# Windowed attention with a gated projection: weights loaded in head order by 64-row transfers, late masks multiplied on GpSimd, and a new fixed order

## The chip, the cores and the metric

The kernel runs on one core of a Trainium2 chip. Five engines work beside each other: TensorE (PE, matrix multiplies; its weight loads are listed as PEld), VectorE (DVE), ScalarE (ACT), GpSimd (POOL) and SyncE (SP, which here issues every DMA). The metric is the device time of one execution in microseconds; the kernel before has a median of 178.93 us over 3 runs (178.68 to 180.42).

## What is computed

Attention over 8 batches, 8 heads, 576 positions and 64 features per head, followed by a gated linear unit and an output projection. Heads 0 to 3 ("plain") look back over 32 positions, heads 4 to 7 ("dilated") over 128 positions at every fourth one.

```python
scores = scale * np.matmul(q, k.transpose(0, 1, 3, 2))
mask_plain = (rel >= 0) & (rel < window)                                          # window = 32
mask_dil = (rel >= 0) & (rel < window * dilation) & (rel % dilation == 0)          # dilation = 4
scores = np.where(masks[None, :, :, :], scores, -1000000000.0)
attn = softmax(scores); attn_out = np.matmul(attn, v)
x = attn_out.transpose(0, 2, 1, 3).reshape(B, S, H * D)                            # 8 x 576 x 512
for k in range(5):
    gate_pre += conv_w[k] * xp[:, k:k + S, :]                                      # causal, per channel
gate = 1 / (1 + exp(-gate_pre))
out = (gate * (x @ w_val)) @ w_out                                                 # 512 x 512 each
```

## The kernel before

The work is cut into 743 tasks with names, and a written list, ORDER, says in which order they are issued and on which engine each runs (P, A, V, G, S for PE, ACT, DVE, POOL, SP). Each engine works through its own share of the list in that order, so a task that waits holds up everything behind it on its engine. HOMES gives each buffer a number, COUNTS how many buffers of a class there are. The list was made ahead of time; nothing is scheduled when the kernel runs.

The names, where b is a batch, g a pair of batches (a group), k a block of a group, cp a half of the 512 channels:

- Loads on SP: Lqp, Lkp, Lvp (plain q, k, v; v in three or four parts), Lqd, Lkd, Lvd (dilated; for batches 0 and 7 q and k have a second piece Lqr, Lkr), Lwv0, Lwv1 and Lwo0, Lwo1 (256 rows of w_val and of w_out each), Lc. Of the large loads only five are under way at once (DEPTH): each waits for the fifth before it to land.
- Tq and Tk (PE, L402 plain, L465 dilated): transposes of q and k; Eq and Ek (ACT or DVE): their copies out of PSUM.
- For each pair of heads and each half of the positions: S (PE, L334) scores for three blocks of 96 queries against 128 keys; E (ACT, L341) the exponential; M (DVE, L348) the multiply with a mask of zeros and ones; then, for both halves, A (PE, L357) the product with v, which has a column of ones beside it, and N (DVE, L366 and L367) the division by the sum.
- U (POOL or ACT): the cast of dilated v (tile vn). HA to HD (POOL or ACT): for batches below NAT = 4 plain v is loaded unshifted, and ten casts per batch write the shifted copies (tile vw).
- Xp (PE, L429) and Xd (PE, L489): transposes back; Fp and Fd: their copies into xT.
- C (PE, L530) the convolution of a block as 80 small matmuls with diagonal matrices; G (ACT, L542) its tanh; V (PE, L550) the product with w_val, 8 matmuls for each half; Y (DVE, L560) gate times value. A group of 1152 positions is cut into 3 blocks of 384, the last group into 4 blocks of 288. C01 is block 1 of group 0, V000 the first half of block 0 of group 0.
- O (PE, L579) the output for 128 positions, EO (ACT or DVE) its copy, ST (SP) its store.
- Wv and Wo (POOL): casts of the weights to bf16 that also put their rows and columns in the order in which the attention leaves its channels. For w_val six tasks of nine casts, most of them 64 rows by 32 or 64 columns; for w_out two tasks of six casts of 32 or 64 rows by 512 columns.

A number behind a P in ORDER puts that many idle multiplies (L664) ahead of a PE task, to keep PE's clock up.

Of the kernel before, what the change touches and what calls it, by code (L numbers as in the profile page):

```python
# [16 lines left out]
0G 16S 19S 17S 34P6 35A 22P 23A 121S 18S 36P1 37V 20S 1S 41P1 50S 38P 24P 39A 40V 51S 25A 54S 52S 53S 26P2 59P  # L17
42A 29P 27A 30A 60A 55G 58G 61A 62P 4S 21A 64V 5G 7G 57G 85S 78P2 86S 79A 31V 117S 120S 43V 44P2 45V 75P 63A
9S 76A 56A 65P 2P 3V 80V 101P4 102V 87S 28V 32P6 103P1 66A 91P 68P 69A 119S 92A 118S 77V 33V 81P 104V 108P 82V
48P 89P 105P 109A 90V 70V 106A 126P 173S 127A 49A 67V 71P2 72V 46P 93P 47V 83P 110V 96P 88A 128V 84V 97A 10G  # L20
8G 6G 174S 98V 73P 123G 125G 122G 129P4 131V 74A 94A 130A 152P 156A 124G 11G 153A 95V 107V 99P 111P 189P 206S
135P 100V 190A 132P 112V 133A 191P 14S 136A 205S 192V 193P1 194A 209S 115P 145P 142P 143A 137V 113P 217P 219A
218A 116A 146A 154P 134V 114V 144V 214P 155V 138P 12S 15G 216A 215V 196P 179P 197A 230P 180A 177P 178A 231A
157P 139V 147V 148P 198V 195V 208S 140P 141A 13G 158V 181P 233P 149V 234A 232V 641P 150P 175S 176G 182A 199P
642A 220P 151V 223P 273S 200V 224A 207S 221A 240S 241S 638P 159P 163A 284P 639V 160A 286A 235V 258P 244P 259V
222V 274S 161P 544S 328S 245V 329S 285A 212G 210G 225V 211G 213G 164P 162V 165V 242S 256P 635P 257V 636A 226P
184P 227V 236P 332P 344P 333V 185A 263P 260P 345A 272S 237V 644P 246P 261A 645V 183V 247V 264A 265V 186V 166P
168P 167A 170A 346P 275S 361S 169V 187P 188V 347A 251P 252A 228P 238P 248P 229A 249A 281P 262V 253V 348P 349A
239A 650P 651A 171P 282A 250V 283V 350V 243G 334P 172V 335A 276S 254P 351P 352A 640S 201P 203P 266P 202A 300P
330S 255V 297P 301A 298A 646S 277G 637S 204V 392S 652S 360S 656P 280G 331G 279G 278G 657A 290P 267V 307P 291A  # L30
311A 308A 353V 268P 369P 270P 269V 302V 354P 271A 370A 371A 424S 355V 299V 336P 337A 363S 647P 653P 303P 654A
648V 292V 304V 339P 340A 287P 396P 659P 288A 289V 660A 397A 393S 312P 394S 408P 293P 366P 338V 410P 364S 368A
409A 341V 313V 309P 367A 294V 411V 305P 310V 306A 398P 342P 343V 415P 416A 412P 643S 413A 399V 649S 665P 666A
362S 365S 429S 382P 414V 372P 385P 386A 417V 387V 395G 425S 668P 373A 669V 661S 430P 383A 428S 431V 356P 478S
418P 432A 295P 357A 427S 426S 384V 419V 375P 376A 433P 296V 435A 662P 663V 388P 389V 449P 434A 446P 450A 495P
358P 451V 403P 447A 314P 667S 477S 404A 496V 448V 374V 377V 316P 315A 317V 378P 379V 318A 359A 400P 401A 390P
452P 402V 453V 436P 391A 437A 493P 494A 319P 510S 439P 509S 497P 440A 481P 438V 454P 320V 482A 518P 498A 520A
515P 516A 664S 519A 677P 517A 542S 479S 658S 405V 441V 455V 499V 442P 678V 674P 576S 483P 480G 541S 406P 443V
675A 575S 484V 534P 535A 500P 671P 380P 511S 501A 488P 485P 407V 536V 670S 584P 672A 486A 585A 381V 502V 543S
420P 586V 489A 444P 503P 521P 421A 531P 445V 422P 532A 522A 504V 547P 533V 548V 423A 321P 323P 514S 322A 325A  # L40
487V 523V 490V 561P 559P 491P 560A 326P 513S 324V 562A 563P 564A 492V 327V 566P 567A 507P 505P 508V 512S 537P
538V 506A 545S 524P 525A 526V 581P 683P 583A 582A 527P 684A 590P 591A 568V 565V 528V 655S 597P 539P 540V 549P
550V 546G 569P 598A 587P 577S 578S 570V 588A 600P 601A 686P 529P 554P 530V 599V 687V 602V 555A 579S 580S 679S
456P 460A 457A 676S 688S 685S 458P 603P 556V 604V 459V 461P 462V 680P 605P 463P 681A 467A 589V 551P 552A 464A
692P 693V 465P 592V 470P 471A 466V 606V 475P 474A 553V 557P 558V 695P 476V 468P 472P 469V 607P 611A 701P 473V
696V 697S 682S 608A 694S 673S 593P 612P 594V 702A 703S 613V 573P 571P 574A 614P 618A 572A 615A 707P 708V 609P
610V 709S 616P 617V 595P 698P 619P 596V 621P 689P 622A 625A 699V 704P 626P 690V 620V 700S 628P 627V 705V 722P
725P 629A 726A 623P 691S 706S 723V 727S 724S 624V 710P 719P 720A 630P 711V 712S 721S 631V 728P 729A 632A 713P
# [7 lines left out]
 'qk': 8,  # L56
 'vp': 2,
 'vd': 2,
 'vn': 2,
 'qT': 4,  # L60
 'kT': 4,
 'et': 5,
 'xn': 4,
 'gate': 4,
 'osb': 5,
 'xT': 3,
 'yT': 3,
 'vw': 2,
 'wt': 3}
DEPTH = 5  # L70
NAT = 4
# [85 lines left out]
def kernel(  # L157
# [10 lines left out]
    nc = tc.nc  # L168
# [429 lines left out]
    def weights():  # L598
# [50 lines left out]
        for pr, parts in enumerate((((0, 64, 0, 0, 0), (64, 64, 0, 0, 1), (0, 32, 1, 96, 0), (32, 32, 1, 64, 0),  # L649
# [5 lines left out]
            def cast_o(eng, t=t, pr=pr, parts=parts):  # L655
                i = wt[t.idx].rearrange("p (c n) -> p c n", c=2)
                for to, n, c, frm, ch in parts:
                    copy(eng, w_out[to:to + n, 2 * pr + c, :], i[frm:frm + n, ch, :])
# [55 lines left out]
```

## Time and profile before

| | |
|---|---|
| median of 3 runs | 178.93 us (178.68 to 180.42) |
| the profiled execution | 179.63 us, of which the span of the core is 177.9 us |
| granted PE clock, mean | 0.988 |
| busy: PE, DVE, ACT, POOL | 151.6, 121.0, 107.0, 53.3 us |
| DMA | 43.70 MB, 246 GB/s on average |

Instructions are told by their line in the kernel before. A window's row gives the busy time of each engine in a stretch of the span; a row of the chain of waits gives start, length and what the chain went through; a group's row gives what was written from what, the shapes, the count, then busy time, the mean in ns of one, and the idle time ahead of it with what ended that.

### The profile page before, as it was taken

To read this page: it belongs to the slowest core of one execution; us is meant where nothing else is said; L and a number is where in the kernel's file an instruction comes from. 1 tells how busy PE (TensorE), PEld (TensorE's weight loads), DVE (VectorE), ACT (ScalarE), POOL (GpSimd) and SP (SyncE) were. 2 spreads that over 40 slices of the span, in tenths; PEclk is the share of its full clock that TensorE was granted. 3 is DMA by queue.
4 is the path that set the end of the run, shared out by engine and by line. 5 is a ranking of instruction groups with operands and counts; after the bars stand their busy time and mean duration, and the time that the engine had idled before them with its cause. 6 is when DMAs were issued, how large, how long until landed. Compare 5 with 4: busy or idle time off the path is not lost.

```text
span 177.9 us, 6891 instructions
## 1 busy us (share of the span) xinstructions
PE 151.6 (85%) x2972; PEld 101.4 (57%) x2996; DVE 121.0 (68%) x249; ACT 107.0 (60%) x174; POOL 53.3 (30%) x121
## 2 busy tenths in 40 slices
PE   6486668888759999886999959989999999999991
PEld 1254356566436667763766747676766557666550
DVE  7023858886926998766789859887997667445430
ACT  2249728688636459777588858886973614422342
POOL 7001979999998345500200003003000000000000
PEclk9999999999978999999999999999999999999999
DMA  4999999999999957699997999979203004513655
GB/s 143 296 369 273 358 338 341 363 347 332 331 314 360 334 187 254 187 344 311 261 306 163 389 348 372 291 211 284 94 4 122 4 0 160 201 63 122 236 199 214
DMA packets 49447, 43.70 MB, mean 246 GB/s; under 512 B 23301, under 2 KB 39685, under 8 KB 49418
## 3 DMA queue, kind: packets, MB, share of 16 engines
q1 hardware_dynamic: 49418, 43.27, 77.5%
q8 instruction: 23, 0.38, 0.9%
q14 instruction: 6, 0.05, 0.1%
HBM read 33.83 MB, written 9.44 MB: 243 GB/s over the span
## 4 chain that ended last, share of the span: by engine, by line
PE 52%; POOL 12%; SPq 9%; DVE 8%; issue 7%; DMA 6%; ACT 4%; POOLq 0%; ACTq 0%; DVEq 0%
PE pu L579 15%; PE pd L550 14%; PE pd L530 7%; DMA wt<-in_moe_w_val_dram 6%; POOL w_val L317 5%; POOL w_out L317 4%; PE pd L357 4%; SPq L301 3%; PE pd L334 3%; POOL vw L317 3%; PE pd L402 3%; PE pu L465 2%; DVE xn L367 2%; PE pu L429 2%; SPq L282 2%
## 5 line engine op out<-in xcount | busy, mean ns | idle before, releaser
L341 ACT ACTIVATE et<-pd 128x576 bf16<-128x576 f32 x64 | 40.3, 653 | 20.5 <-PE pd L334 20.1
L579 PE MATMUL pu<-w_out,yT 128*128 128x512 bf16 x124 | 34.6, 385 | 3.6 <-POOL w_out L317 2.0
L550 PE MATMUL pd<-xT,w_val 128*128 128x384 bf16 (+1 forms) x208 | 35.0, 313 | 0.0
L348 DVE TENSOR_TENSOR et<-et,mask 128x576 bf16<-128x576 bf16 x64 | 31.3, 515 | 2.8 <-ACT et L341 2.7
L367 DVE TENSOR_TENSOR xn<-pd,rec 96x768 bf16<-96x768 f32 x32 | 30.5, 954 | 1.3 <-DVE rec L366 0.2
L542 ACT ACTIVATE gate<-pd 128x768 bf16<-128x768 f32 (+1 forms) x26 | 18.7, 761 | 18.9 <-PE pd L530 14.1
L560 DVE SCALAR_TENSOR_TENSOR yT<-gate,pd 128x768 bf16<-128x768 bf16 (+1 forms) x26 | 22.9, 888 | 9.1 <-PE pd L550 5.9
L550 PEld LDWEIGHTS <-w_val 128*128 128x128 bf16 x208 | 19.4, 97 | 11.9 <-issue 0.9
L317 POOL CAST vw<-vp 32x384 bf16<-32x384 f32 (+2 forms) x37 | 19.8, 536 | 18.2 <-DMA vp<-in_v_dram 16.3
L317 POOL CAST vn<-vd 128x1536 bf16<-128x1536 f32 x6 | 9.0, 1493 | 47.9 <-DMA vd<-in_v_dram 45.0
L334 PE MATMUL pd<-qT,kT 64*128 64x96 bf16 x384 | 17.8, 210 | 5.7 <-issue 1.8
L586 ACT ACTIVATE osb<-pu 128x512 f32<-128x512 f32 x20 | 12.0, 599 | 15.6 <-PE pu L579 15.2
L579 PEld LDWEIGHTS <-yT 128*128 128x128 bf16 x144 | 12.5, 98 | 15.2 <-issue 3.0
L357 PEld LDWEIGHTS <-et 128*128 128x128 bf16 x384 | 15.7, 98 | 9.3 <-issue 5.5
L465 PE MATMUL pu<-ident,qk 128*128 128x128 bf16 x160 | 14.7, 231 | 4.3 <-DMA qk<-in_q_dram 2.5
L334 PEld LDWEIGHTS <-kT 64*128 64x128 bf16 x384 | 10.9, 96 | 13.1 <-issue 6.4
L588 DVE TENSOR_SCALAR osb<-pu 128x512 f32<-128x512 f32 x16 | 11.0, 689 | 8.8 <-PE pu L579 8.0
L465 PEld LDWEIGHTS <-qk 128*128 128x128 bf16 x160 | 10.4, 102 | 9.2 <-DMA qk<-in_q_dram 4.1
L530 PE MATMUL pd<-xT,conv_diag 32*32 32x384 bf16 (+1 forms) x1040 | 14.7, 314 | 0.6 <-DVE xn L367 0.5
L317 POOL CAST w_val<-wt 64x64 bf16<-64x64 f32 (+5 forms) x54 | 13.1, 291 | 1.5 <-DMA wt<-in_moe_w_val_dram 1.3
L366 DVE RECIPROCAL rec<-pd 96x12 f32<-96x12 f32 x32 | 7.2, 223 | 9.1 <-PE pd L357 9.0
L530 PEld LDWEIGHTS <-conv_diag 32*32 32x32 bf16 x1040 | 10.7, 88 | 4.0 <-issue 2.0
(52 smaller groups left out, 161.3 us busy)
## 6 DMA issues: line engine op xcount, KB each, us to landing
out_dram<-osb SPq DMA_DIRECT2D x36, 256.0 KB, 2.3
vd<-in_v_dram SPq DMA_DIRECT2D x8, 768.0 KB, 8.0
vp<-in_v_dram SPq DMA_DIRECT2D x28, 192.0 KB, 6.9
qk<-in_q_dram SPq DMA_DIRECT2D x8, 576.0 KB, 7.9
qk<-in_k_dram SPq DMA_DIRECT2D x8, 576.0 KB, 8.3
qk<-in_q_dram SPq DMA_DIRECT2D x6, 640.0 KB, 6.7
qk<-in_k_dram SPq DMA_DIRECT2D x6, 640.0 KB, 7.3
qk<-in_q_dram SPq DMA_DIRECT2D x2, 512.0 KB, 6.6
```

The source lines that it names most:

```text
L317: nc.gpsimd.tensor_copy(out_, in_)
L334: nc.tensor.matmul(out=ps2[ps.idx][:, l, QB * jj:QB * jj + QB], lhsT=kT[kt.idx][rb, c:c + 128], rhs=qT[qt.idx][rb, c:c + QB], start=True, ...
L341: nc.scalar.activation(out=et[e.idx][:, 0:2 * HW].rearrange("p (l n) -> p l n", l=2), in_=ps2[ps.idx][:, :, 0:HW], func=AF.Exp, scale=scale)
L348: (nc.vector if eng == DVE else nc.gpsimd).tensor_tensor(out=ev, in0=ev, in1=m, op=ALU.mult)
L357: nc.tensor.matmul(out=ps2[po.idx][:, hf, (2 * jj + l) * DA:(2 * jj + l + 1) * DA], lhsT=et[es[hf].idx][:, c:c + 128], rhs=val(j, l), star ...
L367: nc.vector.tensor_tensor(out=xn[xt.idx][0:QB].rearrange("p (h j) l d -> p h (j l) d", h=2), in0=a[:, :, :, 0:D], in1=rr[:, :, :, None].to ...
L465: nc.tensor.transpose(out=o[:, f:f + 128], in_=a[:, c * RD + 128 * cb:c * RD + 128 * cb + 128], identity=ident)
L530: nc.tensor.matmul(out=dst(ps2[pcs[n // 2].idx][G * ob:G * ob + G, n % 2, 0:wd]), lhsT=conv_diag[rb, n, kk, :], rhs=mov(n, rb, c0 + kk - ( ...
L542: nc.scalar.activation(out=gate[gt.idx][:, :, 0:wd], in_=ps2[pc.idx][:, :, 0:wd], func=AF.Tanh, scale=0.5)
L550: nc.tensor.matmul(out=dst(ps2[pv.idx][:, n, 0:wd]), lhsT=w_val[:, mc, c * 128:(c + 1) * 128], rhs=mov(mc, slice(0, 128), c0), start=(mc = ...
L560: nc.vector.scalar_tensor_tensor(out=yT[yb.idx][:, 2 * cp:2 * cp + 2, t0:t0 + wd], in0=gate[gt.idx][:, :, 0:wd], scalar=1.0, in1=ps2[pv.id ...
L579: nc.tensor.matmul(out=ps1[po.idx], lhsT=yT[yb.idx][:, c, c0:c0 + 128], rhs=w_out[:, c, :], start=(c == 0), stop=(c == NCH - 1))
```

## The change

Four things change beside the numbers of the lists.

1. Weights. A 256-row weight load becomes two transfers of 64 rows in two chunks (256 KB each), which put the 64 channels of a head straight into the half of the partitions where they are needed; one of w_out stays a single transfer of 128 rows in two chunks. Six of the seven transfers fill 64 partitions. The casts no longer move rows between halves: w_val takes two tasks of 12 casts over all 128 rows (64 or 128 columns each), w_out two tasks of 5. Wv0 is now on DVE, Wv1 and both Wo on POOL. Loads of weights no longer count among the five large ones. Buffers wt: 3 to 4. The order of the channel halves in the dilated transposes back and in the convolution's weights changes to match.
2. Masks. M of batches 4 to 7 (MP = 4), 32 multiplies, runs on POOL. Buffers et: 5 to 7.
3. Group 0 is cut into 4 blocks, as the last group is.
4. ORDER and HOMES are new throughout. The new list starts with plain k and dilated k of batch 0, and puts the weight loads behind most of the data of batches 0 to 2.

```diff
-            t_m.append(plan.add(f"M{name}", (DVE,), mk, deps=[t_e], tens=[e]))
+            t_m.append(plan.add(f"M{name}", (POOL,) if u // 4 >= MP else (DVE,), mk, deps=[t_e], tens=[e]))
...
-                        nc.tensor.transpose(out=o[64 * hb:64 * hb + 64, f:f + QB],
+                        nc.tensor.transpose(out=o[64 - 64 * hb:128 - 64 * hb, f:f + QB],
...
-        n_blk = 4 if g == B // 2 - 1 else 3
+        n_blk = 4 if g in (0, B // 2 - 1) else 3
...
-        def wload(name, w, pr):
+        def wload(name, w, pr, places):
             t = Ten("wt")
-            def issue():
-                return nc.sync.dma_start(
-                    out=wt[t.idx].rearrange("p (c n) -> p c n", c=2),
-                    in_=src_ap(w, pr * 256 * Dm, [[Dm, 128], [128 * Dm, 2], [1, Dm]]))
-            return t, load(f"L{name}{pr}", t, issue)
+            ls = []
+            for to, n, hs, *c0 in places:
+                def issue(to=to, n=n, hs=hs, c=c0[0] if c0 else 0):
+                    o = wt[t.idx][to:to + n].rearrange("p (c n) -> p c n", c=2)[:, c:c + len(hs), :]
+                    step = hs[-1] - hs[0] or 1
+                    return nc.sync.dma_start(out=o, in_=src_ap(w, hs[0] * D * Dm, [[Dm, n], [step * D * Dm, len(hs)], [1, Dm]]))
+                ls.append(load(f"L{name}{pr}", t, issue, big=False))
+            return t, ls
...
+        for name, w, pr, places in (("wv", moe_w_val, 0, ((0, 64, (0, 1)), (64, 64, (2, 3)))),
+                                ("wv", moe_w_val, 1, ((0, 64, (5, 7)), (64, 64, (4, 6)))),
+                                ("wo", moe_w_out, 0, ((0, 64, (0, 1)), (64, 64, (2, 3)))),
+                                ("wo", moe_w_out, 1, ((0, 128, (4, 6)),))):
+            t, lw = wload(name, w, pr, places)
+
+            def cast_v(eng, t=t, pr=pr):
+                i = wt[t.idx].rearrange("p (c h d) -> p c h d", c=2, d=32)
+                o = w_val[:, 2 * pr:2 * pr + 2, :].rearrange("p c (h d) -> p c h d", d=32)
+                for c in range(2):
+                    copy(eng, o[:, c, 0:4].rearrange("p (h x) d -> p h x d", x=2),
+                         i[:, c, 0:8].rearrange("p (h x) d -> p h x d", x=2)[:, 0:4:2])
+                    copy(eng, o[:, c, 8:12], i[:, c, 8:12])
+                    for x in range(2):
+                        copy(eng, o[:, c, 4 + x:8:2], i[:, c, 3 - x:8:4])
+                        copy(eng, o[:, c, 12 + x:16:2], i[:, c, 13 - x:16:2])
+
+            def cast_o(eng, t=t, pr=pr):
+                i = wt[t.idx].rearrange("p (c n) -> p c n", c=2)
+                copy(eng, w_out[:, 2 * pr, :], i[:, 0, :])
+                for r in range(4):
+                    copy(eng, w_out[G * r:G * r + G, 2 * pr + 1, :], i[G * (r ^ 1):G * (r ^ 1) + G, 1, :])
```

In the new ORDER the engines' own lists read as follows around the points that matter. SP: Lkp0 Lkd0 Lqr0 Lkr0 Lqp0 Lc Lqd0 Lvp0 Lvp0 Lvp0 Lkd1 Lqd1 Lvd0 Lkp1 Lqp1 Lwv0 Lvp1 Lvd1 Lvp1 Lkp2 Lqp2 Lvp1 Lwv1 Lqd2 Lkd2 Lwv1 Lwv0 Lqp3 Lvp2 Lwo1 Lkd3 Lwo0 Lwo0 Lvp2 Lvd2 Lvp2 Lkd4 Lqd3. PE from the first convolution: C00 Ad1 Sp2 Tkd2 Tkd2 C01 Xd1 Sd2 Ap1 Sp2 V000 Tqd2 Ap1 V001 Sd2 Sp2 Xp1 Xd1 Sd2 Sd2 V011 V010 Xp1 Tqp3 Tkd3 C02 O2 Ad2 Sp2 Ad2 Tqd3. POOL: the set-up, HA0 U0 HB0 HC0 U1 HB1 HA1 HD1 HC1 Wv1 Wo1 Wo0 U2 HC2 HB2 HD2 HA2 U3 HD3 HC3 HA3 HB3, then the masks, with U6 among them.

More of the change, by code (lines that the diff above doesn't have):

```diff
@@ L61 @@
  'kT': 4,
- 'et': 5,
+ 'et': 7,
  'xn': 4,
@@ L68 @@
  'vw': 2,
- 'wt': 3}
+ 'wt': 4}
 DEPTH = 5
-NAT = 4
+MP = 4
+NAT = [0, 1, 2, 3]
 def hi_bf16(ap: bass.AP) -> bass.AP:
@@ L613, in conv_e @@
         def conv_e(eng):
[L614 to L617 removed]
+            for to, n, c, frm, ch in ((0, 64, 0, 0, 0), (64, 64, 0, 0, 1), (0, 64, 1, 64, 0), (64, 64, 1, 64, 1),
+                                      (0, 64, 2, 64, 2), (64, 64, 2, 0, 2), (0, 64, 3, 64, 3), (64, 64, 3, 0, 3)):
+                nc.vector.tensor_copy(conv_w[to:to + n].rearrange("p c k -> p (c k)")[:, K * c:K * c + K],
+                                      ps1[pc.idx][frm:frm + n, K * ch:K * ch + K])
             nc.vector.tensor_tensor(
@@ L649, in weights @@
-        for pr, parts in enumerate((((0, 64, 0, 0, 0), (64, 64, 0, 0, 1), (0, 32, 1, 96, 0), (32, 32, 1, 64, 0),
[3 rows of a table removed]
-            t, lw = wload("wo", moe_w_out, pr)
-            def cast_o(eng, t=t, pr=pr, parts=parts):
-                i = wt[t.idx].rearrange("p (c n) -> p c n", c=2)
-                for to, n, c, frm, ch in parts:
-                    copy(eng, w_out[to:to + n, 2 * pr + c, :], i[frm:frm + n, ch, :])
-            tw["out"].append(plan.add(f"Wo{pr}", (POOL,), cast_o, deps=[lw], tens=[t]))
+            ls = []
@@ new lines, in weights @@
+        for name, w, pr, places in (("wv", moe_w_val, 0, ((0, 64, (0, 1)), (64, 64, (2, 3)))),
[14 more added lines that the diff above has]
+            def cast_o(eng, t=t, pr=pr):
+                i = wt[t.idx].rearrange("p (c n) -> p c n", c=2)
+                copy(eng, w_out[:, 2 * pr, :], i[:, 0, :])
+                for r in range(4):
+                    copy(eng, w_out[G * r:G * r + G, 2 * pr + 1, :], i[G * (r ^ 1):G * (r ^ 1) + G, 1, :])
+            val = name == "wv"
+            tw["val" if val else "out"].append(
+                plan.add(f"W{name[1]}{pr}", (POOL, ACT, DVE) if val else (POOL, ACT, DVE), cast_v if val else cast_o, deps=lw,
+                         tens=[t]))
```

90 lines of the change are left out of this document (37 added, 53 removed), and 3 rows, old and new, of the table i.

## The prediction

> **What bounds the kernel now.** I read the windows first, cut at the events that matter, then the chain of waits through the first of them, the timeline of TensorE (PE) where the chain changes engine, and last who releases PE later on.
>
> ```profile
> 0.00:40.46 40.46, 29.23 (x502) 18.26 (x507) 23.66 (x78) 24.00 (x36) 24.18 (x76) 1.00 1.01 314
> 40.46:55.06 14.60, 10.73 (x139) 6.94 (x137) 9.45 (x16) 8.63 (x15) 13.59 (x26) 0.88 1.10 330
> 55.06:130.00 74.94, 68.08 (x1495) 49.37 (x1504) 61.84 (x115) 55.66 (x94) 15.56 (x21) 1.00 0.89 271
> 130.00:170.00 40.00, 39.24 (x829) 25.04 (x832) 25.24 (x41) 15.75 (x25) 0.00 (x0) 1.00 0.28 105
> ```
>
> Columns: the window, its length, busy time of PE, PEld, DVE, ACT, POOL, then PE's granted clock, the DMA share and GB/s. 40.46 is where V000, the first value matmul, starts; 55.06 is where C01, the second block's convolution, starts. From 130 us on PE is full and nothing can be won there without taking PE work away. Between 55 and 130 it is 91% busy. The losses lie before 55: in 40.46 to 55.06 POOL is 93% busy, PE only 73%, and at a clock of 0.88.
>
> ```profile
> 16.77 10.10 DMA wt<-in_moe_w_val_dram
> 27.00 2.45 POOL w_val L317 x9
> ...
> 50.18 0.62 POOL w_out L317
> 50.84 0.58 PE pu L579
> ```
>
> This is the chain (start, length, what). A weight transfer lands at 26.87; POOL casts w_val, the shifted v of batch 1 and w_out without a break until 50.8; only then does the chain pass to PE. The timeline of PE shows the price in its brackets:
>
> ```profile
> 50.84 0.58 PE L579 MATMUL pu<-w_out,yT 128*128 128x512 bf16 x1 [2.02 <-POOL w_out L317]
> ```
>
> 2.0 of the 3.9 us that PE is idle in the second window (14.60 - 10.73) are this wait; the clock of 0.88 takes 12% of 10.73 us of work, 1.3, on top. Together 5.2 us are lost there, of which I count 4.8 to this chain (the rest as the short waits that any stretch has).
>
> **The change part by part.** Costs of PE's tasks, again from the chain, where PE runs without a gap:
>
> ```profile
> 79.44 0.50 PE pd L402 x18
> 85.88 0.86 PE pu L579 x4
> 91.25 0.28 PE pu L465 x5
> 108.55 0.36 PE pd L334 x12
> 111.69 0.38 PE pd L357 x12
> 131.55 1.10 PE pd L530 x80
> 139.17 1.30 PE pd L550 x8
> 149.22 0.98 PE pd L550 x8
> 151.00 0.98 PE pd L530 x80
> ```
>
> By row: a transpose Tp 0.50, an output O 0.86, a transpose Td 0.28, two score tasks S 0.36, an attention-times-v task A 0.38, convolution C 1.10 and value V 1.30 for 384 columns, 0.98 each for 288 columns. For the transposes back, Xd and Xp, I put 0.36, between a pair of S and an A (an estimate).
>
> *Group 0 in four blocks.* C: 4 x 0.98 - 3 x 1.10 = +0.62. V: 8 x 0.98 - 6 x 1.30 = +0.04. The matmuls for heating are 32 in both order lists. **+0.7 us** of PE work.
>
> *The start, up to V000.* What decides is when w_val is ready.
>
> ```profile
> 20.00:60.00 40.00, 31.17 (x631) 21.81 (x636) 29.27 (x52) 24.61 (x39) 36.02 (x89) 0.96 1.10 342
> ```
>
> DMA runs full at 342 GB/s. Sizes follow from the shapes: q or k of a plain batch 0.59 MB, of a dilated one 0.66, dilated v 0.79, a part of plain v 0.20, 256 rows of a weight 0.52. In the old list 7.22 MB are issued up to and with the transfer that landed at 26.87: 7.22 / 0.342 = 21.1, so landing = bytes / 0.342 + 5.8. In the new list the last piece for Wv1 ends 11.02 MB, that for Wv0 11.28, that for Wo0 13.77, and q of dilated batch 3 (Lqd3) 16.26: they land at 38.0, 38.8, 46.1 and 53.3. The weights come much later than before. The casts:
>
> ```profile
> L317 POOL CAST vw<-vp 32x384 bf16<-32x384 f32 x26 | 14.4, 554 | 1.3
> L317 POOL CAST vn<-vd 128x1536 bf16<-128x1536 f32 x6 | 9.0, 1493 | 47.9 <-DMA vd<-in_v_dram 45.0 <-PE pd L357 2.8
> L317 POOL CAST w_out<-wt 32x512 bf16<-32x512 f32 x8 | 5.5, 690 | 0.4
> ...
> L240 POOL TENSOR_SCALAR_AFFINE_SELECT mask<-mask 128x288 bf16<-128x288 bf16 x3 | 1.3, 443 | 0.2 <-DVE mask L237 0.2
> ```
>
> POOL's new list has ten shifts of batch 1 ahead of Wv1 (their v, 9.19 MB, lands at 32.7): 10 x 0.554 = 5.5, to 38.2. Wv1 is 12 casts of 64 or 128 columns by 128 rows, 12 x 0.27 (nine took 2.45 in the chain) = 3.3: 41.5. Wv0, the other 12, go to DVE from 38.8 on, behind a normalisation and two short items; DVE shows no such cast, so from half of POOL's 0.27 to all of it: 41 to 42.5. V000 can start at **41.8** instead of 40.46, +1.3. But more is done ahead of it: one Td, one Tp, two S, one A and a second C, less one Xd: 0.28 + 0.50 + 0.36 + 0.38 + (2 x 0.98 - 1.10) - 0.36 = 2.0. Net **-0.7**. (The work ready before it, behind the k transposes of batch 2 that land at 37.3, ends near 40.0, so PE waits 1.8 us for w_val, within those 41.8.)
>
> *The wait for w_out.* Wo1 (data at 42.6) and Wo0 (46.1) take five casts each: 46.1 + 5 x 0.69 = 49.6. From V000 to O2 the new PE list has four V, one C, four S, two Td, one Tp, one A, two Xp and one Xd, 8.1 us: PE comes to O2 at 49.9. That wait goes, with the cold clock: -4.8. What is late next is Lqd3: an O, two A and an S later, 1.8 us, PE comes to its transpose at 51.7, and the data at 53.3: +1.6. Net **-3.2**.
>
> *The masks of batches 4 to 7.* 32 multiplies leave DVE:
>
> ```profile
> L341 ACT ACTIVATE et<-pd 128x576 bf16<-128x576 f32 x64 | 40.3, 653 | 20.5 <-PE pd L334 20.1
> ...
> L348 DVE TENSOR_TENSOR et<-et,mask 128x576 bf16<-128x576 bf16 x64 | 31.3, 515 | 2.8 <-ACT et L341 2.7
> ```
>
> 32 x 0.515 = 16.5 us of DVE. But who waits for DVE behind 55 us?
>
> ```profile
> PE pd L334 <- issue: 1.8, 1, 1.8
> PE pd L357 <- issue: 1.8, 1, 1.8
> PE pd L357 <- DVE yT L560: 0.6, 2, 0.3
> PE pd L334 <- DVE xn L367: 0.5, 2, 0.4
> ```
>
> 1.1 us in the two largest, of which I take **-0.8**; the two "issue" stalls of 1.8 wait for no engine and stay (either may come or go). On POOL a multiply isn't in the trace. Per element the vn cast has 1.493/1536 = 0.97 ns, the L240 select 443/288 = 1.54 ns, each with one operand; 576 elements give 0.56 and 0.89, and with a second operand read after the first 1.1 to 1.8. I take 1.3, nearer the plain cast. Is there room? From the end of the scores of the first plain mask of batch 4 to the first A of dilated batch 7 the new PE list holds 22 S, 9 Td, 6 Tp, 9 A, 9 O, 6 Xp, 4 Xd, 5 V and 3 C of 384 columns, 34.0 us by the rows above; less 1.0 from scores to mask (0.653 is the exponential of L341), 33.0. POOL has 20 multiplies and a vn cast in it: (33.0 - 1.5) / 20 = 1.58 us for each. At 1.3 it keeps up: **0**. Above 1.58 each multiply's excess counts 20 times.
>
> [...]
>
> **The sum.** +0.7 - 0.7 - 3.2 - 0.8 = -4.0. The profiled execution took 179.63 (span 177.9 and 1.7 around it), the median of the runs is 178.93, 0.7 less: 179.63 - 4.0 - 0.7 = **174.9 us**, 2.3% faster.
>
> **The rivals.**
>
> *Slower: POOL becomes the bound.* Masks above 1.58 us. PE would wait at the A tasks of batches 5 to 7, 80 to 125 us in. For it: two engines hinder each other in this trace, a DVE mask took 1.72, against 0.515 on average, while a POOL cast ran:
>
> ```profile
> 58.55 1.47 POOL L317 CAST vn<-vd 128x1536 bf16<-128x1536 f32 x1 [0.53 <-DMA vd<-in_v_dram]
> ```
>
> ```profile
> 58.61 1.72 DVE L348 TENSOR_TENSOR et<-et,mask 128x576 bf16<-128x576 bf16 x1
> ```
>
> Against it: when POOL has the masks, DVE's operations read one operand from PSUM. At 1.78 us, the upper bound from rows, the gain of 4.0 is just used up; at 2.3 it costs 20 x 0.72 = 14.4: 189. Between, 20 us for each us. Chance 0.18.
>
> *No change, first way: DVE fills before it is relieved.* The masks move only from batch 4 on. From Y000 to Y100 DVE has 8 products, 9 normalisations (L366 and L367), 16 masks and 15 copies of as many columns (I put a mask's 0.515 for each):
>
> ```profile
> L367 DVE TENSOR_TENSOR xn<-pd,rec 96x768 bf16<-96x768 f32 x32 | 30.5, 954 | 1.3 <-DVE rec L366 0.2
> ...
> L366 DVE RECIPROCAL rec<-pd 96x12 f32<-96x12 f32 x32 | 7.2, 223 | 9.1 <-PE pd L357 9.0
> L560 DVE SCALAR_TENSOR_TENSOR yT<-gate,pd 128x576 bf16<-128x576 bf16 x8 | 6.0, 752 | 3.8 <-PE pd L550 3.8
> ```
>
> 8 x 0.752 + 9 x 1.177 + 31 x 0.515 = 32.6 us. PE's work from V000 to V100 (12 Td, 4 Tp, 17 S, 9 A, 5 Xd, 4 Xp, 6 O, 8 V and 2 C of 288 columns, 1 C of 384) is 31.1 by its rows; at the 91% of the window from 55 to 130, and with the wait of 1.6, it takes 35.8. If DVE reaches 93%, as POOL did in the window before, it needs 35.1 and nothing is lost; at its own 83% of 55 to 130 it needs 39.3, 3.5 more: 178.4. Chance 0.10.
>
> *No change, second way: transfers of 64 rows are slow.* Six transfers of 256 KB take 0.77 us each at 342 GB/s; if half the rows meant half the rate, 1.53. Four come before V000 (+3.1), six before Lqd3 (+4.6, all of it felt there): 179.5. The trace has no load over 64 rows, and full queues may fill the gap with their neighbours. [...] Chance 0.10.
>
> **How the numbers follow.** The forecast (0.62) has its own range of 171 to 177: down by 1.8 for an "issue" stall that falls away and by as much if the weights land early, up for half of a rival. A measurement tells about 1% from no change: 177.1 to 180.7. Faster is the forecast and 0.01 of its neighbours, 0.63; same is 0.17 of the two no-change rivals and 0.03 of POOL with masks of 1.69 to 1.87, 0.20; slower is the rest, 0.17. The range of 171.0 to 181.5 leaves out 0.14 above, POOL with masks over 1.9, and 0.05 below.
>
> **What would show it.** V000 at 41 to 43 and no wait for w_out at O2, with PE's clock near 1.00 between 40 and 60; a short wait for q at 52 to 54; POOL's masks at 1.2 to 1.5 us each and A tasks that wait for them less than 2 us in all; DVE near 65% from 80 to 130. Wrong: masks near 2 us with waits "PE pd L357 <- POOL et", loads behind the weights that land 3 to 5 us late, or DVE over 95% from 42 to 78.

## The result, and the profile after

The changed kernel takes 191.75 us (median of 4 runs, 187.67 to 195.23) against 178.81 us for the kernel before on the same chip: slower, ratio 1.0445 with an interval of 1.0297 to 1.0593. In a second set the medians are 191.41 (188.33 to 192.89) and 178.73, ratio 1.057 (1.0451 to 1.0688). The forecast was 174.9, the range 171.0 to 181.5. The ratios leave disturbed executions out and go here by those of 187.67 us and, from a fifth, 186.21 us. The profile shown first is of the longest execution, 195.2 us; a second one, of 190.0 us, is set beside it where it matters.

First the page: the busy times, the 40 slices with PE's granted clock, the queue of instructions, and the masks.

```profile
span 193.5 us, 7085 instructions
...
PE 162.4 (84%) x3092; PEld 107.8 (56%) x3092; DVE 115.2 (60%) x240; ACT 105.2 (54%) x172; POOL 80.4 (42%) x109
...
PEclk9999995795559996999999699996999999999999
...
q8 instruction: 24, 0.39, 0.9%
...
L350 POOL TENSOR_TENSOR et<-et,mask 128x576 bf16<-128x576 bf16 x32 | 40.0, 1273 | 41.8 <-ACT et L343 34.2
```

The masks cost 1.27 us each on POOL, as forecast (1.3), and POOL is not what is full. PE is busy 10.8 us longer than before (162.4 against 151.6), for 0.7 us more work by the forecast's rows: the clock row has 5 to 7 in five of the six slices from 29 to 58 us, where 1.00 was forecast from 40 to 60. The windows, cut at V000 (53.03) and C02 (62.60), answer to those of the prediction:

```profile
0.00:53.03 53.03, 35.74 (x618) 23.40 (x618) 29.44 (x97) 24.86 (x41) 23.51 (x52) 0.85 1.07 283
53.03:62.60 9.57, 9.57 (x126) 7.23 (x124) 8.00 (x16) 4.32 (x8) 8.84 (x14) 0.79 0.90 285
62.60:130.00 67.40, 58.94 (x1274) 41.06 (x1272) 45.08 (x81) 46.21 (x77) 31.63 (x31) 0.95 0.81 252
130.00:193.00 63.00, 58.14 (x1079) 36.11 (x1079) 32.67 (x49) 29.84 (x48) 16.36 (x14) 0.97 0.45 142
```

V000 starts 11.2 us later than forecast. DMA is as full as before (share 1.07) but moves 283 GB/s instead of 314 to 330. Then PE's timeline, of which these are the rows with a bracket over 1.5 us behind 32 us; no other wait of that length is left:

```profile
44.22 0.29 PE L359 MATMUL pd<-vn,et 128*128 128x65 bf16 x2 [3.83 <-issue]
...
52.34 0.29 PE L359 MATMUL pd<-vw,et 128*128 128x65 bf16 x2 [3.21 <-issue]
...
68.20 0.33 PE L467 MATMUL pu<-ident,qk 128*128 128x128 bf16 x3 [2.02 <-issue]
...
74.13 0.52 PE L491 MATMUL pu<-ident,xn 96*64 96x96 bf16 x9 [2.92 <-issue]
...
108.48 1.14 PE L552 MATMUL pd<-xT,w_val 128*128 128x384 bf16 x3 [2.10 <-issue]
...
131.53 0.53 PE L491 MATMUL pu<-ident,xn 96*64 96x96 bf16 x16 [1.93 <-issue]
```

All six are "issue": the next instruction waits for no engine and no load that the profile shows. Together they last 16.0 us, against 1.75 + 1.80 = 3.55 before. The 15.6 us between the two spans are then made up as follows: pauses of this kind +12.4; PE busy for longer +10.8; all other idle time of PE 15.1 instead of 22.8 us, -7.7. Of the 10.8, the forecast's added work is 0.7, and the rest goes with the clock: PE is busy for 25.7 us while the granted clock is 0.5, against 3.2 before, and half of the difference is 11.2 (an estimate, which takes work at half clock to last twice as long: here the 8 products of V000 took 2.10 us at 0.5, those of a later V of 288 columns 1.14 at full clock, a convolution of 288 columns 1.46 and 1.05). In the second profile, 10.4 us longer than before, the same three are +7.1 (pauses of 10.7), +8.1 and -4.9. So the change did take waits away, as meant, and lost more elsewhere.

**What the pauses are.** Queue 8, of kind "instruction" in the page, carries packets of 16,384 bytes, one for each 256 PE instructions (24 packets for some 6,200 instructions). Counting PE's instructions and laying the packets beside them gives this table of the changed kernel, where "C" is how many of the 256 belong to convolutions, and "pause" is how long PE then stands before the next block (counted from the start of its last instruction, so a little longer than the bracket):

```
block entered at  256 issued in   C   packet starts after  took  packet end to next block  pause
      35.97           4.24       160        5.50           1.26           1.49             4.02
      44.22           4.67       160        5.12           1.48           1.51             3.45
      52.33           9.68         0        4.09           1.07           4.57             0.05
      62.06           3.90       160        3.36           1.08           1.71             2.24
      68.20           2.80       160        3.50           1.12           1.30             3.12
      74.13           9.62         0        3.85           1.09           4.90             0.21
      83.96           6.18        83        1.06           1.43           3.69             0.00
      90.15           4.75        77        0.82           1.41           2.52             0.01
```

The packet for the next block doesn't start before PE enters the present one (to within 0.6 us in 71 packets); every pause ends 1.3 to 1.7 us behind the end of a packet. The place of the pauses says the same: number PE's instructions from 0 at the start of the trace, and the multiply behind each of the 40 pauses of this kind over 0.25 us, in this profile and ten of the runs below, has a number that leaves 193 or 194 when it is divided by 256. (The trace of the kernel before lacks 24 of its PE records, and its two leave 184 and 181.) So the next block is there some 2.5 us (packet and 1.4) behind the start of its packet, and PE pauses if it has run through its 256 instructions sooner. In this profile that takes a dense block, one that holds most or all of the 160 short instructions of a convolution, and a late packet. How late goes with the loads under way: over those 71, of the kernel before, the changed one and the first experiment, the start came 0.35 us + 0.39 x the time that the loads then issued still took to land (correlation 0.90): 0.3 us on average with nothing queued, 3.2 with 6 to 8 us queued. That is a correlation, not yet a cause.

**What the narrow transfers do.** A load of weights takes longer from issue to landing, though it has half the bytes (the page's DMA issues, changed and before):

```profile
wt<-in_moe_w_val_dram SPq DMA_DIRECT2D x4, 256.0 KB, 10.3
```

```profile
wt<-in_moe_w_val_dram SPq DMA_DIRECT2D x2, 512.0 KB, 8.1
```

Windows from 36 to 40 us, of the changed kernel and of the kernel before:

```profile
36.00:40.00 4.00, 4.00 (x126) 2.79 (x123) 1.88 (x4) 3.50 (x7) 2.51 (x5) 0.92 1.10 173
```

```profile
36.00:40.00 4.00, 3.41 (x88) 2.41 (x86) 3.48 (x6) 3.28 (x6) 3.67 (x7) 1.00 1.11 344
```

With the same share of busy DMA engines (1.10 and 1.11) 173 GB/s are moved instead of 344 while the 64-row transfers are under way. Between 36 and 41 us packets of 2,048 bytes take 209 ns on average (97 in the kernel before), and the 60 packets of 1,024 bytes of other loads between them 113 ns (53 in the kernel before, from 24 to 51 us). Landing minus bytes / 0.345 grows from 5.5 us at the last load ahead of Lwv1 to 11.4 behind Lwo0. This is the rival that was given 0.10. The rate is half, as that rival supposed; why it is half, no trace shows.

### The profile page after: what moved, and what is told of

It is laid out like the page before. It is cut to its first block, busy times and chain, and to the rows that moved or that the text cites. A ratio compares the mean times of both kernels' runs of the same rounds, so it can differ in the third digit from the quotient of the medians.

```text
span 193.5 us, 7085 instructions
## 1 busy us (share of the span) xinstructions
PE 162.4 (84%) x3092; PEld 107.8 (56%) x3092; DVE 115.2 (60%) x240; ACT 105.2 (54%) x172; POOL 80.4 (42%) x109
## 4 chain that ended last, share of the span: by engine, by line
PE 70%; issue 9%; DVE 9%; DMA 6%; ACT 3%; SPq 1%; ACTq 0%; DVEq 0%
PE pd L552 18%; PE pu L581 17%; PE pd L532 8%; PE pd L336 6%; PE pd L359 6%; PE pd L404 5%; PE pu L467 4%; PE pu L491 3%; DMA qk<-in_q_dram 3%; DMA qk<-in_k_dram 3%; DVE xn L369 3%; PE pu L431 2%; DVE et L350 2%; DVE qT L317 1%; PE pd L669 1%
## 5 line engine op out<-in xcount | busy, mean ns | idle before, releaser
L350 POOL TENSOR_TENSOR et<-et,mask 128x576 bf16<-128x576 bf16 x32 | 40.0, 1273 | 41.8 <-ACT et L343 34.2
L552 PE MATMUL pd<-xT,w_val 128*128 128x288 bf16 (+1 forms) x224 | 38.8, 321 | 2.2 <-issue 2.1
L581 PE MATMUL pu<-w_out,yT 128*128 128x512 bf16 x144 | 37.5, 395 | 0.0
L562 DVE SCALAR_TENSOR_TENSOR yT<-gate,pd 128x576 bf16<-128x576 bf16 (+1 forms) x28 | 23.4, 837 | 18.8 <-PE pd L552 18.5
L552 PEld LDWEIGHTS <-w_val 128*128 128x128 bf16 x224 | 21.9, 103 | 14.7 <-issue 4.0
L544 ACT ACTIVATE gate<-pd 128x576 bf16<-128x576 f32 (+1 forms) x28 | 18.8, 720 | 11.0 <-PE pd L532 10.7
L588 ACT ACTIVATE osb<-pu 128x512 f32<-128x512 f32 x22 | 13.3, 603 | 16.3 <-PE pu L581 15.6
L350 DVE TENSOR_TENSOR et<-et,mask 128x576 bf16<-128x576 bf16 x32 | 16.8, 545 | 5.0 <-ACT et L343 5.0
L467 PEld LDWEIGHTS <-qk 128*128 128x128 bf16 x160 | 10.8, 105 | 9.2 <-DMA qk<-in_k_dram 3.6
L532 PE MATMUL pd<-xT,conv_diag 32*32 32x288 bf16 (+1 forms) x1120 | 15.9, 314 | 0.0
L315 ACT COPY xT<-pu 128x576 bf16<-128x576 bf16 x18 | 11.6, 643 | 7.6 <-PE pu L431 4.4
L336 PEld LDWEIGHTS <-kT 64*128 64x128 bf16 x384 | 10.7, 98 | 7.7 <-issue 2.9
L404 PE MATMUL pd<-ident,qk 128*64 128x128 bf16 x288 | 12.4, 243 | 2.2 <-DMA qk<-in_q_dram 0.8
```

Source lines behind the costliest of these rows:

```text
L336: nc.tensor.matmul(out=ps2[ps.idx][:, l, QB * jj:QB * jj + QB], lhsT=kT[kt.idx][rb, c:c + 128], rhs=qT[qt.idx][rb, c:c + QB], start=True, ...
L350: (nc.vector if eng == DVE else nc.gpsimd).tensor_tensor(out=ev, in0=ev, in1=m, op=ALU.mult)
L404: nc.tensor.transpose(out=o[64 * y:64 * y + 64, 128 * j:128 * j + 128], in_=a[:, (y * PJ + j) * D:(y * PJ + j + 1) * D], identity=ident)
L467: nc.tensor.transpose(out=o[:, f:f + 128], in_=a[:, c * RD + 128 * cb:c * RD + 128 * cb + 128], identity=ident)
L532: nc.tensor.matmul(out=dst(ps2[pcs[n // 2].idx][G * ob:G * ob + G, n % 2, 0:wd]), lhsT=conv_diag[rb, n, kk, :], rhs=mov(n, rb, c0 + kk - ( ...
L552: nc.tensor.matmul(out=dst(ps2[pv.idx][:, n, 0:wd]), lhsT=w_val[:, mc, c * 128:(c + 1) * 128], rhs=mov(mc, slice(0, 128), c0), start=(mc = ...
```

## The experiments

Two theories stood against each other: the width of the transfers, and the instruction fetch. "Changed" is the changed kernel; each time is compared with the kernel before in the same set, whose medians were 180.34 (the first four), 178.73, 179.09, 179.92 and 179.04.

**Width.** Changed, with each 64-row transfer made as one of 128 rows:

```diff
-                    o = wt[t.idx][to:to + n].rearrange("p (c n) -> p c n", c=2)[:, c:c + len(hs), :]
...
+                    c = to // 64
+                    return nc.sync.dma_start(out=wt[t.idx][:, c * Dm:(c + 1) * Dm],
+                                             in_=src_ap(w, (4 * pr + 2 * c) * D * Dm, [[Dm, 128], [1, Dm]]))
```

> The changed kernel with each of its six 64-row weight transfers replaced, in its place, by one of 128 rows and one chunk: the same 256 KB, count and order. The rows of w_val and w_out then lie in another order in SBUF, so the output is that of permuted weights; nothing else differs. Theory 1 (width): transfers into 64 partitions move at half rate and hold up the loads behind them; in the changed kernel the loads fell some 6 us further behind the bytes between 32 and 51 us. Then here landing minus bytes/0.345 stays between 5 and 6.5 us up to Lqd3, V000 starts at 42 to 46 us instead of 53.0, and the time is 178 to 183 us. Rival (instruction fetch alone): the loads land earlier, but the pauses of PE that wait for nothing the profile shows (16.0 us in six pauses) remain, and the time stays at 186 to 190.

187.82 us, ratio 1.0503 (1.0404 to 1.0603). The same window shows the full rate again, and landing minus bytes / 0.345 stays between 4.3 and 4.9 us from Lvp1 to Lkd4:

```profile
36.00:40.00 4.00, 4.00 (x40) 2.26 (x37) 1.77 (x4) 2.93 (x6) 3.85 (x14) 0.52 1.10 341
```

But the time is the rival's. The medians differ by 3.6 us (191.41 to 187.82), and the ratio lies between the two of the changed kernel, 1.0445 and 1.057, so no gain can be told. The pauses are still there:

```profile
47.89 0.24 PE L359 MATMUL pd<-vw,et 128*128 128x65 bf16 x2 [2.52 <-issue]
...
61.88 0.33 PE L467 MATMUL pu<-ident,qk 128*128 128x128 bf16 x3 [1.66 <-issue]
...
68.34 0.56 PE L491 MATMUL pu<-ident,xn 96*64 96x96 bf16 x9 [3.47 <-issue]
```

The half rate is shown and is repaired here; it is the smaller part. V000 starts at 48.4, later than the 42 to 46 expected: behind the pause of 2.52, and behind 10.2 us at half clock from 29.6 on, after a wait of 1.66 for DVE's mask at 27.3.

**Width, in the kernel before.** Its loads cut into two halves of 64 rows:

```diff
+                for h in range(2):
+                    r = nc.sync.dma_start(
+                        out=wt[t.idx][64 * h:64 * h + 64].rearrange("p (c n) -> p c n", c=2),
+                        in_=src_ap(w, (pr * 256 + 64 * h) * Dm, [[Dm, 64], [128 * Dm, 2], [1, Dm]]))
```

> The kernel before with each of its four weight loads made as two transfers of 64 rows, one for each half of the partitions; same bytes, same place, same buffers. Theory 1 (width at half rate): each load costs 1.5 us more of DMA time, so the loads fall 6 us behind by 43 us; POOL's casts of w_val start 1.5 us later, those of w_out 4 to 6 us later, PE waits that much longer at the first output: 181 to 186 us. Rival (the queues fill the gap with neighbours): within 1 us of the kernel before.

183.1 us, ratio 1.0206 (1.0124 to 1.0288). The time is in the theory's range, by another route than the one expected: PE's wait of 2.02 us for w_out isn't longer but gone. The loads are late (250 GB/s from 36 to 45 us, 336 in the kernel before), and so are the instructions: the packet for the block entered at 37.42 starts 5.6 us after it instead of 3.3, and a pause of 2.74 us stands at 43.38 where the kernel before had none. Here too the narrow transfers made the loads under way last longer, and the fetch came later with them.

**Borders of the blocks.** The idle multiplies of 512 columns are cut, which moves all later borders:

```diff
-            nc.tensor.matmul(out=o, lhsT=warm[:, 0:128], rhs=warm, start=True, stop=True)
+            for x in range(0, 512, 256):
+                nc.tensor.matmul(out=o[:, x:x + 256], lhsT=warm[:, 0:128], rhs=warm[:, x:x + 256], start=True, stop=True)
```

> The kernel before with each idle multiply made as two of 256 columns: 64 PE instructions more, all of them before 45 us, the same columns. Theory 2 (instruction fetch): PE's instructions come in blocks of 256 (16 KB on queue 8), one block ahead; a block is asked for when PE enters the one before it and is there 4 to 8 us later when DMA is busy, so PE pauses where it runs through 256 instructions faster than that. Where the borders of the blocks fall then decides: replaying the trace of before with borders 64 instructions earlier gives 10 us of pauses instead of 3.6 to 6, so 182 to 187 us with the half clock that follows pauses of 2 us. Rival (the pauses belong to the data, not to the borders): 178 to 180 us, the pauses at the same tasks as before.

184.09 us, ratio 1.023 (1.0112 to 1.0348). The time is in the range of the theory, its reason isn't borne out: the profile has two pauses of 2.24 and 2.02 us, at other tasks than before (77.8 and 101.5), 4.3 us and not 10. The replay had put every delay at 3.5 us; with the delay by the queue it gives 5.5.

The changed kernel likewise, in four of 128 columns:

> The changed kernel with each idle multiply made as four of 128 columns: 192 PE instructions more, all but a few before 45 us, the same columns. Theory 2 (instruction fetch): replaying the trace of after with borders 192 instructions earlier gives 8.4 us of pauses instead of 14 to 16, so 180 to 185 us against the 187 to 195 of the changed kernel, with pauses at other tasks. Theory 1 alone: no change, 187 to 190, loads as late as in the changed kernel. In both the loads stay 6 us behind between 32 and 51 us.

190.4 us (changed: 191.4): missed. Pauses 11.9 us, not 8.4. With the narrow transfers two packets start 6.9 and 6.1 us late, more than the replay had allowed. Both misses led to the rule with the queue's length, on which the later shift rests.

**The dense blocks themselves.** Two taps of five:

```diff
-                for kk in range(K):
+                for kk in range(K - 2, K):
```

> The kernel before with two of the five taps of the convolution: each convolution task is 64 PE instructions instead of 160 (the gate is that of two taps). PE's work falls by 0.6 of 13.8 us, 8.3. Theory 2 (the dense convolutions outrun the instruction fetch): the two pauses of 1.75 and 1.80 go as well: 166 to 171 us. Rival (pauses with another cause): 170 to 172.

170.3 us (169.54 to 171.62): 8.4 less than the kernel before, of which PE's work is 8.3 by the rows. The time lies in both ranges and decides nothing; both pauses went, and hardly anything was won beyond the work.

> The changed kernel with 128-row weight transfers (rows in another order, as in the experiment on width) and two of the five taps of the convolution: 64 PE instructions for each convolution instead of 160. PE's work falls by 8.6 us. Theory 2: the pauses of 10.2 us and the half clock behind them go with the dense blocks, so 187.8 falls to 164 to 171, level with or below the kernel before with two taps. Rival (the new order is slow for another reason, such as waits for data): 187.8 - 8.6 = 179, and 7 to 9 us above the kernel before with two taps.

169.06 us (167.69 to 174.06): 18.8 less than with five taps, of which PE's work is 8.6 by the rows. Neither of the two has a pause of PE over 0.25 us that is "issue", and behind 44 us the clock stays full; the clock row of the page with the new order:

```profile
PEclk9999999557999999999999999999999999999999
```

The ratios to the full kernel before are 0.9522 (0.9441 to 0.9604) and 0.94 (0.9302 to 0.9497): without dense blocks the new order is level with the old one or ahead of it. So the new order is 7.5 us slower with five taps, and with two it is no longer slower (1.2 us faster, which the intervals don't tell from nothing). A rival that is slow for another reason, at 179, is out.

**Changed, once more.**

> The changed kernel once more, unaltered, beside the others of this set, because its first times lie far apart (186.2 to 195.2). Both theories: 186 to 195. Theory 2 (instruction fetch): each pause of PE for which the profile names no releaser ends 1.3 to 1.7 us after a packet on queue 8 ends, as all six did in its first profile, and falls in a block of 256 instructions that PE runs through in under 5 us. Rival (such pauses have another cause): ends that lie anywhere.

191.41 us (188.33 to 192.89). The profile is of the 190.0 us execution:

```profile
40.51 0.24 PE L359 MATMUL pd<-vn,et 128*128 128x65 bf16 x2 [1.64 <-issue]
...
49.17 0.29 PE L359 MATMUL pd<-vw,et 128*128 128x65 bf16 x2 [3.96 <-issue]
...
70.25 0.56 PE L491 MATMUL pu<-ident,xn 96*64 96x96 bf16 x9 [3.31 <-issue]
...
126.34 0.53 PE L491 MATMUL pu<-ident,xn 96*64 96x96 bf16 x16 [1.77 <-issue]
```

Each pause ends 1.4 to 1.6 us behind the end of a packet, and stands behind a block issued in 5.7, 4.5, 3.0 and 3.7 us (the first a little over the 5 expected, with a packet 4.6 us late). The sum of the pauses varies from execution to execution, 10.7 us here and 16.0 in the first.

**The best shift.** Changed with 128-row transfers, and the first 24 idle multiplies in four:

> The changed kernel with 128-row weight transfers (rows in another order), and 24 of its 32 idle multiplies each made as four of 128 columns: 144 PE instructions more before 45 us, the same columns. Theory 2 with a fetch delay of 0.35 us + 0.39 x the time that the loads under way still take: the replay of the trace of the kernel without this edit gives 10.2 us of pauses at its own borders and 5.5 us with the borders 144 instructions earlier, the least of all shifts: pauses at 46, 63 and 115 us, and 181 to 184 us instead of 187.8. Rival (borders don't matter): 187 to 189 us, pauses at 45, 60, 65 and 122 us.

182.56 us, ratio 1.0265 (1.017 to 1.036), 5.3 below the kernel without the cuts, by an edit that only adds instructions:

```profile
45.62 0.68 PE L532 MATMUL pd<-xT,conv_diag 32*32 32x288 bf16 x42 [1.60 <-issue]
...
64.62 0.70 PE L532 MATMUL pd<-xT,conv_diag 32*32 32x288 bf16 x27 [2.63 <-issue]
...
116.71 0.34 PE L532 MATMUL pd<-xT,conv_diag 32*32 32x384 bf16 x3 [0.60 <-issue]
```

The pauses stand where they were expected, 4.8 us in all instead of 10.2. Hardly anything else of PE's time changed between the two profiles, whose spans are 180.5 and 185.8 us: PE is busy for 160.5 us in both, its other idle time is 15 us in both, and the clock is 0.5 for 20.5 us in both. So the 5.3 us are the pauses alone, and it is the borders that moved them: this is the sharpest test. What remains above the forecast of 174.9 is mostly the clock (some 8 us by the estimate above); 10.2 of the 20.5 us at half clock begin at 29.8, behind a wait of 1.65 us for DVE's mask and ahead of any pause.

**A shorter queue.** `DEPTH = 3` instead of 5.

> The changed kernel with 128-row weight transfers (rows in another order) and three large loads under way at once instead of five. Theory 2: over 71 fetches of three kernels the delay from PE's entering a block to the start of the fetch of the next was 0.35 us + 0.4 x the time that the loads then under way still took to land (0.3 us with none, 3.2 with 6 to 8 us). With three large loads that time falls from 6 to 8 us to about 4, the delay from 3.3 to 2, each pause by some 1.3: pauses 4 to 6 us instead of 10.2, and 180 to 184 us instead of 187.8. Rival (the delay is not from the queued loads, or fewer loads under way cost as much as they bring): 187 us or more, delays still 3 us.

184.57 us, ratio 1.0208 (1.0087 to 1.0329): faster, as forecast, but the reason given isn't seen. In its profile, of the longest of its four executions, the delays at the dense blocks are mostly 3 to 4 us and the pauses 10.1 us in all, as without the edit. The edit didn't shorten what it was meant to shorten: at the blocks entered between 20 and 125 us the loads under way still took 5.4 us on average to land, against 5.5 without it. The delays follow that time in this profile too (slope 0.40, correlation 0.83), so the rule is neither refuted here nor tested. Why the shorter executions gain stays open.

> The kernel before with three large loads under way at once instead of five, nothing else. Theory 2: in the kernel before, PE pauses twice for its instructions, 1.75 and 1.80 us, with fetch delays of 3.8 and 3.5 us while 7 us of loads were queued; with three large loads the delays fall to about 2.5 and the pauses to under 1 each: 176 to 178.5 us. Rival (as with three loads in the changed kernel, whose profile showed delays of 3 to 4 us still: the queue is not what three large loads shorten, and loads come later): 179 to 183 us, pauses and delays as before.

179.33 us against 179.92, ratio 1.0088 (1.0014 to 1.0162): no gain. Two pauses of 1.34 us remain, delays of up to 4.1 us, and PE waits 2.45 us for w_out. The rival was right; here too the queue was hardly shorter, with 5.1 us on average until the loads under way at a block's start had landed (20 to 125 us).

**The masks alone, in the old order.**

```diff
-            t_m.append(plan.add(f"M{name}", (DVE,), mk, deps=[t_e], tens=[e]))
+            t_m.append(plan.add(f"M{name}", (POOL,) if u // 4 >= 4 else (DVE,), mk, deps=[t_e], tens=[e]))
```

> The kernel before with the 32 masks of batches 4 to 7 on GpSimd, nothing else changed (the order list differs in those 32 letters alone, 5 et buffers). The prediction's terms alone: masks of 1.27 us, no wait of PE for them, 0.8 us less of waits for DVE: 177.5 to 179 us. Rival (a mask that takes 0.75 us longer delays the product with v behind it, since this order leaves no room for it): PE waits at A tasks between 75 and 135 us for GpSimd, 181 to 186 us.

190.15 us (185.75 to 191.89) against 179.09: 11 more at the medians, and 6.7 more in the shortest execution, which is the profiled one. The waits (engine, line, releaser, us in all, times, longest) name POOL, for the masks and for the casts queued behind them:

```profile
PEld L357 <- POOL et L348: 7.9, 6, 2.5
PE pd L357 <- POOL vn L317: 7.1, 4, 2.9
PE pd L357 <- POOL et L348: 5.7, 5, 2.4
```

Not one pause of the kind "issue" over 0.25 us is left here, though PE's list of instructions, and so every border, is that of the kernel before: PE, held up by POOL, takes 8.0 us for the block that it ran through in 4.6 to 4.7 us in the runs above that kept this list, and its packet is there in time. That fits the fetch.

**The masks back on DVE, in the new order** (`MP = 8` and 32 letters of the list, on the kernel with the best shift).

> The kernel of the experiment with shifted borders (128-row weight transfers with rows in another order, 24 idle multiplies in four; 182.56 us), with the 32 masks of batches 4 to 7 back on DVE; order otherwise as it is. Between 75 and 130 us PE is 97% busy there, DVE 42.2 of 55 us, and 26 of the masks fall there: at 0.515 us they add 13.4 us to DVE, 55.6 in 55. So if the move of the masks is what lets PE run full in this order, DVE becomes the bound: 186 to 192 us, with waits of PE for DVE between 80 and 130. Rival (the prediction's term: the relief of DVE is worth 0.8 us): 182.5 to 184.

185.92 us against 182.56, ratio 1.0484 (1.0348 to 1.0621) against 1.0265: the move is worth 3.4 us there (the intervals of the two ratios just overlap), between the two expectations. PE's waits for masks grow:

```profile
PEld L359 <- DVE et L350: 6.0, 7, 1.9
PE pd L359 <- DVE et L350: 4.1, 4, 1.6
```

and from 75 to 130 us PE is busy 50.19 of 55 us with the masks on DVE, 53.57 with them on POOL, 49.27 in the kernel before (windows of the three kernels in this order: masks on DVE, masks on POOL, before):

```profile
75.00:130.00 55.00, 50.19 (x1037) 34.68 (x1035) 47.80 (x90) 39.29 (x65) 1.47 (x1) 1.00 0.83 248
```

```profile
75.00:130.00 55.00, 53.57 (x1152) 37.60 (x1150) 42.15 (x73) 42.41 (x68) 32.14 (x26) 1.00 0.85 254
```

```profile
75.00:130.00 55.00, 49.27 (x1083) 35.62 (x1088) 44.63 (x86) 41.95 (x71) 4.55 (x3) 1.00 0.93 277
```

**A version with every row in place.** Four of the six narrow transfers as 128 rows of two separate heads, with the shift and three large loads:

```diff
+                    lo, hi = places[0][2][c], places[1][2][c]
+                    return nc.sync.dma_start(out=wt[t.idx][:, c * Dm:(c + 1) * Dm],
+                                             in_=src_ap(w, lo * D * Dm, [[(hi - lo) * D * Dm, 2], [Dm, 64], [1, Dm]]))
```

> A version with everything in its right place: the changed kernel with the 64-row transfers of Wv0 and Wo0 made as 128-row transfers of one chunk each (the source takes heads 0 and 2, then 1 and 3; the two of Wv1 stay at 64 rows), three large loads under way at once, and the 24 idle multiplies in four. Theory 1 and 2 together: of the 3.6 us that width costs in all, 2.4 come back, the shift brings 4 to 6 us and the shorter queue about 3: 178 to 183 us against 188 to 191 for the changed kernel. If it beats the kernel before, below 178. Rival (none of the three adds to another): 184 to 187.

194.31 us, worse than changed. PE's timeline has a wait of 8.1 us for w_out:

```profile
70.15 1.44 PE L581 MATMUL pu<-w_out,yT 128*128 128x512 bf16 x3 [8.13 <-POOL w_out L319]
```

and in the window from 50 to 60 us little is moved:

```profile
50.00:60.00 10.00, 9.04 (x127) 6.93 (x128) 8.99 (x22) 3.21 (x6) 3.34 (x5) 0.83 0.30 95
```

DMA moves 95 GB/s at a share of 0.30, though packets of 2,048 bytes take their usual time (a median of 84 ns, 88 in the kernel before). So few packets were under way at once: from 50 to 60 us mostly 2 of 2,048 bytes at a time. Each of the four new transfers changes its semaphore 3 times (the second of Wv0 at 38.4, 49.4 and 50.5 us), the other weight transfers of this run 16 times. In the experiment on width the transfers of the same size into the same 128 partitions, with 128 rows in one piece as source, change theirs 16 times. The source's first dimension of 2 is the author's guess at what decides; it was not shown, as the edit was not run by itself. No version faster than the kernel before was found.

## Why the prediction was wrong

The step that failed is the one that put a price on the pauses: **"the two 'issue' stalls of 1.8 wait for no engine and stay (either may come or go)"**. They were taken as fixed, and no rival made them grow. They are PE waiting for its instructions, and the change alters three things that bear on them: where 256-instruction borders fall (shown: moving the borders alone took 5.4 us of them away), how dense the blocks are (shown: without dense blocks they go), and how late a packet starts, which goes with the loads under way (a correlation, and later packets wherever transfers were narrow). In place of the 0 of the sum stand +7.1 to +12.4 us of pauses (10.7 and 16.0 in the two profiles, 3.55 before) and, beside them, a PE that is busy 8.1 to 10.8 us longer, nearly all of it for the clock by the estimate above; the two together are more than the whole loss, and the other waits fell by 4.9 to 7.7 us.

- *Group 0 in four blocks, +0.7.* By the rows PE's work rose by that; no run measures it by itself. What the step left out: one convolution more, 160 instructions, and dense blocks in the stretch where loads are queued for 6 to 8 us.
- *V000 at 41.8.* It came at 53.0: two pauses, 7.0 us, stand between C00 and it, and the last 9.5 us before it are at half clock. With full-width loads it is 48.4. The forecast also had w_val ready by 42.5 at the latest, as if DVE were free when Wv0 lands; it landed at 42.0, but the normalisation ahead of the cast on DVE waits for a product of PE that came behind the first pause, and the cast ran from 47.0 to 50.1.
- *The wait for w_out goes, with the cold clock, -4.8; then a wait for Lqd3, +1.6.* The wait for w_out did go, and no wait for Lqd3 came, since PE was late itself. The cold clock did not go: the granted clock is 0.5 for 30.7 us, in windows of 3.4 us or a multiple, against 3.4 us in the kernel before (50.9 to 54.3). In these two profiles each window opens in, or up to 0.7 us behind, a pause or wait of 1.8 us or more; not each of these is followed by one, and in other runs one opens in or behind a wait of 1.2 to 1.4 us, so when the clock falls stays open.
- *Masks on POOL at 1.3, no wait for them: 0.* Right: 1.27, and PE waits for one of them for 0.2 us at most. The term holds for the new order only; in the old one the same move costs 6.7 to 11 us.
- *DVE relieved, -0.8.* The sign is right and the size too small: 3.4 us in the new order. The two largest waits for DVE in the kernel before don't measure what a full DVE costs another order.
- *Rival, transfers of 64 rows at half rate, 0.10.* It was there (173 GB/s instead of 344 from 36 to 40 us), with the price of 4.6; by landing minus bytes 6 us were lost. On the whole time of the changed kernel it weighs 3.6 us at the medians, which the ratios don't tell from nothing; in the kernel before, narrow transfers cost 2%. Its route is partly another than argued: the instruction packets come later too (5.1 to 5.5 us behind the entry into the block instead of 3.3).
- *Rivals POOL as the bound and DVE full before its relief.* Neither shows in the new order: PE's waits for POOL's masks are all but nil, and DVE is busy 54% of 40 to 60 us and 58% of 60 to 80.

What the profile of before offered and the prediction didn't use: both "issue" pauses ended 1.5 to 1.7 us behind a packet of the queue of kind "instruction", which the page of that profile lists, in its third part, with 23 packets:

```profile
q8 instruction: 23, 0.38, 0.9%
```

```profile
84.61 0.20 PE L357 MATMUL pd<-vw,et 128*128 128x65 bf16 x1 [1.75 <-issue]
...
105.56 0.26 PE L334 MATMUL pd<-qT,kT 64*128 64x96 bf16 x4 [1.80 <-issue]
```

## What to carry to other kernels

Take a pause whose releaser is "issue", in the middle of a full PE, for a fetch until shown otherwise: set the packets of the instruction queue beside the count of PE's instructions, and look for stretches that issue 256 instructions in less than the fetch takes with the loads under way there. Here that was some 6 us: about 3.4 until the packet starts, 1.1 for it, 1.5 behind it. The time hung on where the borders fell: 144 extra idle instructions moved it by nearly 3% (187.82 to 182.56 us). So price a new order with its blocks laid out, and keep dense tasks out of stretches with many loads queued. Transfers into 64 partitions moved at half rate here (173 GB/s instead of 344) and slowed other loads under way, so count their bytes twice.

## What the runs showed that was not expected

- In none of the 71 packets were instructions fetched further ahead than one block, even while DMA was idle: the packet started when the block before was entered (to within 0.6 us), 0.3 us later on average with nothing queued and 3 to 7 with the loads of these kernels. What holds the packet up behind the loads was not measured.
- The half-rate transfers also halved the rate of packets of other loads under way (1,024 bytes in 113 ns instead of 53).
- One execution of the changed kernel differs from another by 9 us (186.21 to 195.23), and its profiles differ in the sum of pauses (10.7 and 16.0 us) and in the time at half clock (23.9 and 30.7 us).
